# Block-sparse attention with token mix: inner units in pairs with shared keys, edge units of both blocks and four heads, key copies on GpSimd

## The chip, the cores and the metric

The kernel runs on one core of a Trainium2 chip. The metric is the device time of one execution in microseconds (us). Engines are named as in the profile: PE is TensorE, PEld its weight loads, DVE is VectorE, ACT is ScalarE, POOL is GpSimd, SP is the engine that only issues transfers. SBUF is the on-chip memory, PSUM holds the results of PE.

## The reference

Attention over 4 batches, 8 heads, 768 rows in 24 blocks of 32, with a mask by blocks; its result goes through a token mix of dense products.

```python
def _attn_ref(q, k, v, sampled_blocks):          # [4, 8, 768, 64]
    scores = scale * np.matmul(q, k.transpose(0, 1, 3, 2))
    mask = np.abs(blk_i - blk_j) <= 1
    mask = mask | (blk_i == 0) | (blk_j == 0) | (blk_i == 23) | (blk_j == 23)
    for qb in range(24):                         # three sampled blocks for each block of rows
        for kb in sampled_blocks[qb]:
            mask[qb * 32:(qb + 1) * 32, kb * 32:(kb + 1) * 32] = True
    scores = np.where(mask, scores, -1e9)
    attn = np.exp(scores - np.max(scores, axis=-1, keepdims=True))
    attn = attn / (np.sum(attn, axis=-1, keepdims=True) + 1e-09)
    return np.matmul(attn, v)

def _moe_ref(x, w_theta, w_tok_r, w_tok_i, w_ch):   # x: [4, 768, 512]
    theta = x @ w_theta
    yr = np.einsum('ts,bsd->btd', w_tok_r, x * np.cos(theta))
    yi = np.einsum('ts,bsd->btd', w_tok_i, x * np.sin(theta))
    u = x + yr + yi
    return u + np.maximum(u @ w_ch, 0.0)
```

The arrays of the mix arrive as 64-bit words, which the kernel decodes to two float parts each.

## The kernel before

The two batch pairs bp (two batches b each, eight heads as four p and two e) go through attention one after the other. Attention is a list of units. For each bp there are 8 edge units (named w; tiles SW, PW, Tw, XW), whose rows are the first or last block and see all 768 keys, one for each batch, head parity e and edge block z (four heads each); and 22 inner units, one for each other block i. An inner unit covers two batches and eight heads and sees eight key blocks: its own three neighbours, the two edge blocks and three sampled ones.

An inner unit runs through these steps, which the loop over units staggers:

- `gather_k`: copies eight key blocks out of the resident keys kb to the tile kg, scaled by -0.125. ScalarE copies the blocks of the window (L235), VectorE the three sampled ones, at addresses that it reads from a table (L224, L244).
- `scores` (L288): 16 products of 64 rows by 32 columns on PE to S in PSUM, then two reductions to m on VectorE (L291).
- `weights` (L300): four exponentials to P on ScalarE.
- `turn` (L307, L309): eight transpositions to T on PE, and a copy to pT on ScalarE.
- `values` (L318): 32 products of 128 rows by 32 columns to X, 16 with va (the values of the window and of block 0, loaded by SP, L263) and 16 with vb (the sampled values, gathered row by row by an indirect transfer from POOL, L270, and the last block). PE runs each product of full-precision floats as two passes, so the profile counts each twice.
- `finish` (L325 to L328): division by the sum, and a store to xs in DRAM (L341).

Between these, `Decoder` puts one third of a weight piece into each unit: L63 and L80 on ScalarE, L67 to L84 on VectorE. Engines run their instructions in the order written; attention's order is written out by hand in the loop at the end of `attention`. kg has two buffers, vb three, va two, P, pT and X two, T one. `token_mix` begins when attention ends: it reads xs back (xa, xr), and PE bounds it.

Of the kernel before, what the change touches and what calls it, by code (L numbers as in the profile page):

```python
# [12 lines left out]
I32 = mybir.dt.int32  # L13
# [10 lines left out]
VB_BUFS = 3  # L24
Q_AHEAD = 4
# [91 lines left out]
class Tables:  # L117
# [6 lines left out]
    def make(self, nc, cp):  # L124
# [11 lines left out]
        nc.gpsimd.tensor_copy(qi, iota_i)  # L136
        first_i = cp.tile([96, NP], I32, name="first_i")
# [17 lines left out]
        self.rows = rows = cp.tile([96, NP, NB], I32, name="rows")  # L155
# [7 lines left out]
        nc.vector.tensor_scalar(rows, base, ZEROS, None, op0=ALU.add)  # L163


def attention(tc, qT, qE, kT, vr, sampled, xs, ident, pieces, follow):
# [9 lines left out]
    with ExitStack() as ctx, ExitStack() as early:  # L176
# [11 lines left out]
        ps_x = ctx.enter_context(tc.tile_pool(name="ps_x", bufs=2, space=PSUM))  # L188
# [5 lines left out]
        kgs = [gp.tile([P, 8, 8, 32], F32, name=f"kg{x}") for x in range(2)]  # L194
        vas = [cp.tile([P, 1040], F32, name=f"va{x}") for x in range(2)]
# [3 lines left out]
        def load_q(bp, i):  # L199
            if i % 2 == 0:  # L200
                return
            t = qp.tile([P, 2, 2, 4, 32], F32, tag="q", name=f"q{bp}_{i}", bufs=Q_BUFS)
            nc.sync.dma_start(t.rearrange("r u b p f -> r u (b p f)"), qT[bp][:, i - 1 : i + 1, :])
            qbs[bp, i], qbs[bp, i + 1] = t[:, 0], t[:, 1]

        def load_k(bp, b, p0=0, n=4, queue=nc.sync):
            if (b, p0) == (0, 0):
                kbs[bp] = kp.tile([P, 8, NB, 32], F32, tag="kb", name=f"kb{bp}")
            queue.dma_start(kbs[bp][:, 4 * b + p0 : 4 * b + p0 + n], kT[bp, b][:, p0 : p0 + n])

        def load_edges(bp):
            raw = ep.tile([P, 512], F32, tag="qw", name=f"qw{bp}")
            nc.sync.dma_start(raw, qE[bp])
            qes[bp] = raw

        def turn_edges(bp):
            t = ep.tile([P, 2, 2, 4, 32], F32, tag="qe", name=f"qe{bp}")
            nc.vector.tensor_scalar(t.rearrange("r z b p f -> r (z b p f)"), qes[bp], -0.125, None, op0=ALU.mult)
            qes[bp] = t
# [3 lines left out]
        def number_blocks(bp, i):  # L223
            _, numbers[bp, i] = nc.values_load_multi_w_load_instructions(  # L224
                tab.block[0:1, 3 * i : 3 * i + 3], engines=[mybir.EngineType.DVE], min_val=0, max_val=NB - 1,
                skip_runtime_bounds_check_because="Tables clamps the block numbers",
            )

        def gather_k(bp, i):
            kg, kb = kgs[i % 2], kbs[bp]  # L230
            def blocks(b0, n):
                return kb[:, :, b0 : b0 + n, :].rearrange("r g s f -> r s g f")

            def copy(s0, b0, n):
                nc.scalar.activation(kg[:, s0 : s0 + n], blocks(b0, n), AF.Copy, scale=-0.125)  # L235

            if i <= 2:
                copy(3, 0, 1)
                copy(7, NB - 1, 1)
            for b0, n in fresh(i, i <= 2):  # L240
                copy(b0 % 3, b0, n)
            for k, number in enumerate(numbers.pop((bp, i))):
                src = kb[:, :, bass.ds(number, 1), :].rearrange("r g s f -> r s g f")
                nc.vector.tensor_scalar(kg[:, 4 + k : 5 + k], src, -0.125, None, op0=ALU.mult)  # L244
            st[bp, i] = dict(kg=kg)

        def fresh(i, new):

            runs = []
            for blk in range(i - 1 if new else i, i + 2):  # L250
                if runs and blk % 3:
                    runs[-1][1] += 1
                else:
                    runs.append([blk, 1])
            return runs

        def load_window(bp, i):
            va = vas[i % 2]
            if i <= 2:
                nc.sync.dma_start(va[96:128], vr[768 * bp : 768 * bp + 32])  # L260
            for b0, n in fresh(i, i <= 2):
                s0 = 32 * (b0 % 3)
                nc.sync.dma_start(va[s0 : s0 + 32 * n], vr[768 * bp + 32 * b0 : 768 * bp + 32 * (b0 + n)])  # L263
            st[bp, i]["va"] = va

        def gather_v(bp, i):
            vb = vbs[i % VB_BUFS]
            if i <= VB_BUFS:
                nc.sync.dma_start(vb[96:128], vr[768 * bp + 736 : 768 * bp + 768])
            nc.gpsimd.indirect_dma_start(  # L270
                out=vb[0:96],
# [4 lines left out]
            st[bp, i]["vb"] = vb  # L276

        def scores(bp, i):

            s = st[bp, i]  # L280
            q = qbs.pop((bp, i))
            kg = s["kg"]
            sc = ps_s.tile([P, 2, 2, 256], F32, tag="S", name=f"S{bp}_{i}")
            for b in range(2):
                for p in range(4):
                    for e in range(2):
                        rows = slice(64 * e, 64 * e + 64)
                        nc.tensor.matmul(sc[32 * p : 32 * p + 32, e, b, :], q[rows, b, p, :], kg[rows, :, 4 * b + p, :], start=True, stop=True)  # L288
# [13 lines left out]
        def turned(pts, name):  # L302

            n = len(pts)
# [3 lines left out]
            out = wp.tile([P, 8, 128], F32, tag="pT", name=f"pT{name}")  # L308
            nc.scalar.copy(out[:, :n], t[:, :n])  # L309
            return out  # L310

        def turn(bp, i):
            s = st[bp, i]
            s["T"] = turned([s["P"][:, e, b, 128 * c : 128 * c + 128] for c in range(2) for e in range(2) for b in range(2)], f"{bp}_{i}")
# [400 lines left out]
```

## Time and profile before

| | |
|---|---|
| time, median of 3 runs | 638.25 us (636.85 to 638.58) |
| span of the profiled execution | 635.0 us |
| its mean granted clock of PE | 0.964 |
| PE busy over the span | 563.2 us (89%) |
| VectorE | 463.5 us (73%) |
| ScalarE | 361.0 us (57%) |
| GpSimd | 45.6 us (7%) |
| moved by DMA | 96.52 MB, mean 152 GB/s |
| last inner unit's turning copy starts | 286.1 us |

The profile has no time of its own for the execution but its span; the span lies 3.25 us under the median of the runs. A line of groups reads: source line, engine, operation, out<-in, shapes, count, then busy us, mean ns of one, idle us of the engine ahead of it with what ended that. A line in order of time reads: start, us, engine, line, operation, count. Windows are given in us from the start of the span, with busy time and count of each engine, granted clock of PE, share of the 16 DMA engines and GB/s.

### The profile page before, as it was taken

The numbers are of one execution on the slowest core, as the hardware profiler recorded it, in microseconds if no ns is written. First come the engines' busy times: TensorE is split into PE (matmuls) and PEld (weight loads), VectorE is DVE, ScalarE is ACT, GpSimd is POOL, SyncE is SP. The second block draws the span as 40 slices with busy tenths as digits, with TensorE's granted clock in tenths as the row PEclk, the third lists the DMA queues.
The fourth block names the chain that finished last, engine by engine and source line by source line (L and its number), as shares of the span: only waits on it lengthen the run. The fifth ranks groups of instructions, "written<-read, shape, count | busy, mean of one in ns | idle before, by whom it ended". The sixth has DMA issues, their size and how long they took to land.

```text
span 635.0 us, 19148 instructions
## 1 busy us (share of the span) xinstructions
PE 563.2 (89%) x7808; PEld 483.1 (76%) x7808; DVE 463.5 (73%) x1239; ACT 361.0 (57%) x774; POOL 45.6 (7%) x56
## 2 busy tenths in 40 slices
PE   4987778769887768668999999999999999999997
PEld 1555545545455546547999999999999999999997
DVE  1897978875798878758999697575973767746554
ACT  1586768764587767656667564355642465524520
POOL 0101212211002211110000000000000000000000
PEclk9998989988898999887999999999999999999999
DMA  8859979999778997866542224211241211211002
GB/s 287 259 156 246 275 209 259 258 278 345 219 204 244 251 257 226 221 161 170 139 130 73 64 84 143 69 47 50 80 124 59 70 51 42 80 59 61 27 1 99
DMA packets 79959, 96.52 MB, mean 152 GB/s; under 512 B 5312, under 2 KB 64832, under 8 KB 79488
## 3 DMA queue, kind: packets, MB, share of 16 engines
q1 hardware_dynamic: 73088, 72.99, 39.2%
q0 software_dynamic: 4928, 17.57, 10.7%
q10 hardware_dynamic: 1856, 4.74, 2.1%
q8 instruction: 61, 1.00, 0.7%
q14 instruction: 26, 0.21, 0.1%
HBM read 82.70 MB, written 12.58 MB: 150 GB/s over the span
## 4 chain that ended last, share of the span: by engine, by line
PE 66%; DMA 18%; DVE 8%; issue 4%; ACT 2%; SPq 1%; DVEq 1%; ACTq 0%
PE y L555 10%; PE y L556 10%; PE y L557 10%; DMA va<-in_vr_dram 10%; PE X L318 4%; PE S L288 4%; PE T L307 4%; PE h L519 3%; PE h L518 3%; PE o L578 3%; PE h L517 3%; PE o L580 3%; PE o L579 3%; DMA kb<-in_kT_dram 3%; PE SW L357 2%
## 5 line engine op out<-in xcount | busy, mean ns | idle before, releaser
L300 ACT ACTIVATE P<-S,m 128x256 f32<-128x256 f32 x176 | 69.0, 477 | 15.1 <-DVE m L291 14.9
L307 PEld LDWEIGHTS T<-ident,P 128*128 128x128 f32 x352 | 42.1, 150 | 38.2 <-ACT P L300 25.9
L307 PE MATMUL T<-ident,P 128*128 128x128 f32 x352 | 60.5, 304 | 11.2 <-ACT P L300 6.1
L318 PE MATMUL X<-va,pT 128*32 128x65 f32 (+1 forms) x1408 | 50.3, 233 | 21.9 <-DMA va<-in_vr_dram 18.1
L291 DVE TENSOR_REDUCE m<-S 128x2 f32<-128x512 f32 x88 | 56.7, 686 | 16.7 <-PE S L288 9.8
L309 ACT COPY pT<-T 128x1024 f32<-128x1024 f32 x44 | 44.8, 1018 | 41.5 <-PE T L307 41.4
L288 PE MATMUL S<-kg,q 64*32 64x256 f32 x1408 | 55.1, 404 | 10.9 <-issue 10.9
L555 PE MATMUL y<-w_tok_r_hi,zh 128*128 128x384 f32 x192 | 64.6, 336 | 0.0
L556 PE MATMUL y<-w_tok_r_lo,zh 128*128 128x384 f32 x192 | 64.4, 335 | 0.0
L557 PE MATMUL y<-w_tok_r_hi,zl 128*128 128x384 f32 x192 | 64.3, 335 | 0.0
L556 PE MATMUL y<-w_tok_i_lo,zh 128*128 128x384 f32 x192 | 64.2, 334 | 0.0
L555 PE MATMUL y<-w_tok_i_hi,zh 128*128 128x384 f32 x192 | 64.2, 334 | 0.0
L557 PE MATMUL y<-w_tok_i_hi,zl 128*128 128x384 f32 x192 | 62.7, 334 | 0.0
L270 POOL DMA_INDIRECT vb<-in_vr_dram,rows x44 | 44.1, 1002 | 229.3 <-PE X L318 206.0
L318 PEld LDWEIGHTS X<-va,pT 128*32 128x32 f32 (+1 forms) x1408 | 35.6, 116 | 31.8 <-DMA va<-in_vr_dram 17.8
L517 PE MATMUL h<-w_theta_hi,xTh 128*128 128x256 f32 x192 | 55.8, 290 | 1.9 <-ACT xTh L508 1.9
L519 PE MATMUL h<-w_theta_hi,xTl 128*128 128x256 f32 x192 | 55.6, 290 | 0.5 <-DVE xTl L509 0.5
L518 PE MATMUL h<-w_theta_lo,xTh 128*128 128x256 f32 x192 | 55.3, 288 | 0.0
L318 PE MATMUL X<-vb,pT 128*32 128x65 f32 (+1 forms) x1408 | 49.8, 232 | 5.0 <-issue 5.0
L521 ACT ACTIVATE t<-h,up_int 128x256 f32<-128x256 f32 x48 | 22.7, 473 | 42.7 <-PE h L519 42.0
L528 ACT ACTIVATE cs<-rr 128x256 f32<-128x256 f32 x48 | 20.0, 416 | 45.8 <-DVE rr L526 45.8
L578 PE MATMUL o<-uh,w_ch_hi 128*128 128x384 f32 x128 | 42.5, 336 | 0.9 <-DVE of L584 0.9
(125 smaller groups left out, 1337.2 us busy)
## 6 DMA issues: line engine op xcount, KB each, us to landing
xa<-xs SPq DMA_DIRECT2D x192, 64.0 KB
va<-in_vr_dram SPq DMA_DIRECT2D x30, 260.0 KB
xr<-xs SPq DMA_DIRECT2D x24, 256.0 KB
out_dram<-of SPq DMA_DIRECT2D x32, 192.0 KB
q<-in_qT_dram SPq DMA_DIRECT2D x22, 256.0 KB
xs<-xo SPq DMA_DIRECT2D x44, 128.0 KB
vw<-in_vr_dram SPq DMA_DIRECT2D x6, 780.0 KB
raw_tok_r<-in_w_tok_r_dram SPq DMA_DIRECT2D x9, 512.0 KB
```

The lines of the kernel that those rows point to most:

```text
L288: nc.tensor.matmul(sc[32 * p : 32 * p + 32, e, b, :], q[rows, b, p, :], kg[rows, :, 4 * b + p, :], start=True, stop=True)
L291: nc.vector.tensor_reduce(m[:, e], sc[:, e], axis=AX.X, op=ALU.min)
L300: nc.scalar.activation(pt[:, e, b, :], sc[:, e, b, :], AF.Exp, bias=m[:, e, b : b + 1], scale=-1.0)
L307: nc.tensor.transpose(t[:, k, :], pt, ident)
L318: nc.tensor.matmul(x[32 * p : 32 * p + 32, g, :], pt[0:rows, k, 32 * p : 32 * p + 32], v[0:rows, v0 + 65 * p : v0 + 65 * p + 65], start=st ...
L517: nc.tensor.matmul(ps, hi[:, c, :], wh[:, c, :], start=c == 0, stop=False)
L518: nc.tensor.matmul(ps, hi[:, c, :], wl[:, c, :], start=False, stop=False)
L519: nc.tensor.matmul(ps, lo[:, c, :], wh[:, c, :], start=False, stop=c == 3)
L555: nc.tensor.matmul(acc, zh[:, dd], wh[:, j, tt], start=j == 0 and m == 0, stop=False)
L556: nc.tensor.matmul(acc, zh[:, dd], wl[:, j, tt], start=False, stop=False)
L557: nc.tensor.matmul(acc, zl[:, dd], wh[:, j, tt], start=False, stop=j == 5 and m == 1)
L578: nc.tensor.matmul(ps, wh[:, c, :], uh, start=c == 0, stop=False)
```

## The change

Inner units are taken in pairs (i odd, i+1). Four key blocks are shared by the pair: blocks 0, 23, i and i+1. Each unit keeps four of its own: the neighbour that the pair doesn't share and the three sampled ones. kg becomes one tile with two places for shared blocks (used in turn by pairs) and two for own ones (one for each unit of a pair). All key copies go to POOL as plain copies; the scale moves to q (L217, VectorE). The values of a pair are 16 times three products: for each of two units 32 columns with its vb (now 128 gathered rows: sampled blocks and the neighbour), then one product of 64 columns with the shared va. They run once for a pair, in the iteration of the next pair's first unit, and are normalised and stored once for a pair. pT is one tile for both units, without a second buffer; xo has one buffer, vb four; X is two PSUM banks.

An edge unit now has both edge blocks and four heads of one batch: four units for each bp instead of eight. Their scores are products of 64 rows by 64 columns, their values products of 128 rows by 64 columns.

xs is laid out by unit and half of the heads, so that a store writes 2 KB runs; a tile xr is then read by four transfers. Keys are loaded in four parts from SP, for the second batch pair as well. Decoding is spread by weights, two for an edge unit and one for an inner unit.

```diff
+        kg = gp.tile([P, 4, 4, 8, 32], F32, name="kg")
+        pT = gp.tile([P, 2048], F32, name="pT")
...
+        def scale_q(bp, i):
+            if i % 2:
+                t = qbs[bp, i].rearrange("r u b p f -> r (u b p f)")
+                nc.vector.tensor_scalar(t, t, -0.125, None, op0=ALU.mult)
...
         def gather_k(bp, i):
-            kg, kb = kgs[i % 2], kbs[bp]
...
-                nc.scalar.activation(kg[:, s0 : s0 + n], blocks(b0, n), AF.Copy, scale=-0.125)
...
-                nc.vector.tensor_scalar(kg[:, 4 + k : 5 + k], src, -0.125, None, op0=ALU.mult)
+            kb, u, a = kbs[bp], (i - 1) % 2, ((i - 1) // 2) % 2
+            def copy(dst, blocks):
+                nc.gpsimd.tensor_copy(dst, blocks.rearrange("r g s f -> r s g f"))
+
+            if u == 0:
+                if i <= 3:
+                    copy(kg[:, a, 0:2], kb[:, :, 0 : NB : NB - 1, :])
+                copy(kg[:, a, 2:4], kb[:, :, i : i + 2, :])
+            near = i + 1 if u else i - 1
+            copy(kg[:, 2 + u, 3:4], kb[:, :, near : near + 1, :])
+            for k, number in enumerate(numbers.pop((bp, i))):
+                copy(kg[:, 2 + u, k : k + 1], kb[:, :, bass.ds(number, 1), :])
...
+        def load_pair(bp, i):
+            if i % 2 == 0:
+                return
+            va = vas[((i - 1) // 2) % VA_BUFS]
...
+            nc.sync.dma_start(va[64:128], vr[768 * bp + 32 * i : 768 * bp + 32 * (i + 2)])
...
         def gather_v(bp, i):
-                out=vb[0:96],
+                out=vbs[(i - 1) % VB_BUFS],
...
+        def values(bp, i):
+            x = st[bp, i]["X"] = sums_tile(f"{bp}_{i}")
+            va = vas[((i - 1) // 2) % VA_BUFS]
+            order = [(b, e, p) for b in range(2) for e in range(2) for p in range(4)]
+
+            def weigh(b, e, p, c, u0, n, v, start, stop):
+                r0 = 64 * (p % 2) + 32 * u0
+                v0 = 65 * (8 * b + 4 * (p // 2) + 2 * e + p % 2)
+                nc.tensor.matmul(
+                    x[r0 : r0 + 32 * n, b, 2 * (p // 2) + e, :], pT_pair[:, 4 * c + 2 * e + b, p, u0 : u0 + n, :], v[:, v0 : v0 + 65],
+                    start=start, stop=stop,
+                )
+
+            for b, e, p in order:
+                for u in range(2):
+                    weigh(b, e, p, 1, u, 1, vbs[(i - 1 + u) % VB_BUFS], True, False)
+                weigh(b, e, p, 0, 0, 2, va, False, True)
...
+        def values_wide(bp, b, pp, e):
...
+            for c in range(2):
+                for k in range(6):
+                    v0 = 130 * e + 65 * c
+                    nc.tensor.matmul(
+                        x[64 * c : 64 * c + 64, b, 2 * pp + e, :], pT_wide[:, e, k, 64 * c : 64 * c + 64], v[:, k, v0 : v0 + 65],
+                        start=k == 0, stop=k == 5,
+                    )
...
-            nc.sync.dma_start(xr[b, j].rearrange("r i c u -> r i (c u)"), xs[b // 2, b % 2, 4 * j : 4 * j + 4].rearrange("i r c -> r i c"))
+            for p in range(4):
+                src = xs[b // 2, 4 * j : 4 * j + 4, p % 2, :, b % 2, p // 2].rearrange("i q c -> q i c")
+                nc.sync.dma_start(xr[b, j][32 * p : 32 * p + 32].rearrange("r i c u -> r i (c u)"), src)
```

PE, before, around the values of unit 11 of the first batch pair. A row is line, operation, out<-in and the shape of the product's output (rows, which are columns on the array, by 65), xN for N in a row:

```order
L288 MATMUL S_13_1687<-kg_117,q_13_1391 32x256 x16
L307 MATMUL T_12_1707<-ident,P_12_1625 128x128 x8
L318 MATMUL X_11_1727<-va_119,pT_11_1623 32x65 x4
L318 MATMUL X_11_1727<-vb_122,pT_11_1623 32x65 x4
L318 MATMUL X_11_1727<-va_119,pT_11_1623 32x65 x4
```

Now, at the values of the pair 11 and 12 (the three rows of X come 16 times):

```order
L300 MATMUL T_12_1442<-ident,P_12_1378 128x128 x8
L282 MATMUL S_14_1476<-kg,q_13_1128 32x256 x16
L335 MATMUL X_11_1496<-vb_122,pT 32x65
L335 MATMUL X_11_1496<-vb_123,pT 32x65
L335 MATMUL X_11_1496<-va_119,pT 64x65
L335 MATMUL X_11_1496<-vb_122,pT 32x65
```

Groups of four products of one width have become runs of two of 32 and one of 64, and the values stand between the scores and the turning, once for two units.

VectorE, before, from the end of unit 11 to the reduction of unit 14 (ISA rows set an address, TENSOR_LOAD reads block numbers):

```order
L325 TENSOR_SCALAR sm_11_1762<-X_11_1727 128x4
L326 RECIPROCAL sm_11_1762<-sm_11_1762 128x4
L328 TENSOR_TENSOR xo_11_1765<-X_11_1727,sm_11_1762 128x256
L244 ISA
L244 TENSOR_SCALAR kg_117<-kb_131 128x256
L244 ISA
L244 TENSOR_SCALAR kg_117<-kb_131 128x256
L244 ISA
L244 TENSOR_SCALAR kg_117<-kb_131 128x256
L224 TENSOR_LOAD sb_block
L291 TENSOR_REDUCE m_14_1800<-S_14_1783 128x2 x2
```

Now, the same engine at that place:

```order
L217 TENSOR_SCALAR q_15_1293<-q_15_1293 128x512
L285 TENSOR_REDUCE m_14_1493<-S_14_1476 128x2 x2
L75 TENSOR_SCALAR ds_tok_r_1560<-da_tok_r_1420 128x512
L77 SCALAR_TENSOR_TENSOR raw_tok_r_1230<-raw_tok_r_1230,ds_tok_r_1560 128x512
L315 TENSOR_SCALAR sm_11_1563<-X_11_1496 128x8
L316 RECIPROCAL sm_11_1563<-sm_11_1563 128x8
L319 TENSOR_TENSOR xo_11_1566<-X_11_1496,sm_11_1563 128x512
L285 TENSOR_REDUCE m_15_1601<-S_15_1584 128x2 x2
```

The key copies and table reads have left VectorE, a scaling of q has come in ahead of the reduction, and the normalisation stands there once for a pair at twice the width.

POOL, before, in an inner stage has only gathers:

```order
L270 DMA vb_121<-in_vr_dram,rows 96x1040
L270 DMA vb_122<-in_vr_dram,rows 96x1040
L270 DMA vb_120<-in_vr_dram,rows 96x1040
L270 DMA vb_121<-in_vr_dram,rows 96x1040
L270 DMA vb_122<-in_vr_dram,rows 96x1040
```

Now, for the first unit of a pair:

```order
L265 DMA vb_121<-in_vr_dram,rows 128x1040
L243 COPY kg<-kb_128 128x512
L243 COPY kg<-kb_128 128x256
L243 ISA
L243 COPY kg<-kb_128 128x256
L243 ISA
L243 COPY kg<-kb_128 128x256
L243 ISA
L243 COPY kg<-kb_128 128x256
L233 TENSOR_LOAD sb_block
L265 DMA vb_122<-in_vr_dram,rows 128x1040
```

Five copies and a table read have moved in between two gathers, each of which has grown from 96 to 128 rows.

296 lines of the change are left out of this document (157 added, 139 removed).

## The prediction

> **What bounds the kernel now.** I read the span cut at its stages first, because the change touches attention alone.
>
> ```profile
> core 0: us, PE busy (x) PEld busy (x) DVE busy (x) ACT busy (x) POOL busy (x), PEclk, DMA share, GB/s
> 0.00:8.45 8.45, 0.00 (x0) 0.03 (x1) 0.60 (x6) 1.49 (x2) 1.46 (x12) 1.00 0.65 190
> 8.45:43.50 35.05, 33.71 (x576) 17.09 (x576) 25.02 (x64) 19.74 (x31) 2.93 (x3) 1.00 0.80 263
> 43.50:145.60 102.10, 77.57 (x2161) 51.69 (x2153) 81.97 (x218) 73.08 (x149) 19.81 (x19) 0.95 0.91 247
> 145.60:180.70 35.10, 30.65 (x699) 19.22 (x697) 27.42 (x54) 21.55 (x34) 2.74 (x3) 0.90 0.78 261
> 180.70:286.70 106.00, 79.86 (x2208) 55.47 (x2208) 83.06 (x225) 73.84 (x151) 18.62 (x19) 0.91 0.86 227
> 286.70:635.00 348.30, 341.42 (x2181) 339.64 (x2176) 245.46 (x675) 171.27 (x410) 0.00 (x0) 0.99 0.26 78
> ```
>
> The rows are: waiting for keys, edge units of batch pair 0, its 22 inner units, edge units of pair 1, its inner units, token mix. The mix is TensorE at 98%; I leave its 348.3 us alone. In the inner stages (208 us) no engine is above 80%, and the DMA engines are at 86 to 91%. So I read the length of an inner unit from the 22 turning copies of each batch pair, and the chain of waits for what ends last.
>
> ```profile
> L309 ACT COPY pT<-T x22: 1012/1012/1043, 45.5 to 147.6; 128x1024 f32<-128x1024 f32 x22
> L309 ACT COPY pT<-T x22: 1005/1012/1055, 182.6 to 286.1; 128x1024 f32<-128x1024 f32 x22
> ...
> by line: DMA va<-in_vr_dram 24.9%; PE S L288 12.1%; PE X L318 11.9%; PE T L307 8.7%; DMA xs<-xo 8.5%; DMA kb<-in_kT_dram 7.5%; issue 7.5%; DMA raw_tok_r<-in_w_tok_r_dram 5.3%; DVE m L291 3.1%; DVE mw L359 1.5%; PE SW L357 1.3%; PE Tw L307 1
> ```
>
> 102.1 and 103.5 us over 21 steps each: 4.9 us a unit, 9.8 us for two. The chain (52 to 175 us) gives a quarter to the load of the window's values (va). The DMA queues between 90 and 130 us say how full they are:
>
> ```profile
> DMA packets 5068, 9.40 MB, mean 235 GB/s; under 512 B 563, under 2 KB 2778, under 8 KB 5057
> q1 hardware_dynamic: 4161, 6.05, 52.5%
> q0 software_dynamic: 896, 3.20, 31.8%
> ```
>
> These 40 us are 4.1 pairs of units: q1 costs 5.1 us a pair at 288 GB/s, the gather q0 3.1 us at 252 GB/s; 8.2 of 9.8 us. TensorE's part of a unit, once in order of time and once around the changes of product shape:
>
> ```profile
> 95.06 0.30 PE L318 MATMUL X<-va,pT 128*32 128x65 f32 x8
> 95.17 0.30 PE L318 MATMUL X<-vb,pT 128*32 128x65 f32 x8
> 95.40 1.09 PE L288 MATMUL S<-kg,q 64*32 64x256 f32 x32
> ...
> 99.68 1.09 PE L288 MATMUL S<-kg,q 64*32 64x256 f32 x32
> 100.70 1.09 PE L307 MATMUL T<-ident,P 128*128 128x128 f32 x8
> 100.98 0.82 PE L307 MATMUL T<-ident,P 128*128 128x128 f32 x6
> 101.73 0.32 PE L318 MATMUL X<-va,pT 128*32 128x65 f32 x8
> 101.86 0.30 PE L318 MATMUL X<-vb,pT 128*32 128x65 f32 x8
> 101.98 0.30 PE L318 MATMUL X<-va,pT 128*32 128x65 f32 x8
> ...
> L307 PE MATMUL T<-ident,P x176: 272/273/474, 43.5 to 147.1; 128*128 128x128 f32 x176
> L318 PE MATMUL X<-va,pT x88: 217/220/245, 101.7 to 111.9; 128*32 128x65 f32 x88
> ```
>
> Start to start: scores 1.02 us, turning 1.03 us, and the values in groups of four products (two passes each, so x8) every 0.113 us; eight groups and the way back to scores make 1.04. TensorE works 3.1 of 4.9 us. The four products of a group share one 0.113 us because they sit on four different column groups.
>
> **The change, part by part.**
>
> *Values (X), the term that decides.* Before, a pair of units is 16 groups: 2.1 us. Now it is 16 times (two 32-column products, then one 64-column product): 32 steps, and at each the width on the array changes. No row shows 32 beside 64 columns. Bounds:
> - Below: the width costs nothing, and the 64-column product of one head runs beside the 32-column products of the next (other half of the columns): 17 steps of 0.113 = 1.9 us, a gain of 0.2.
> - Above: a change of shape costs what it costs in the rows. T to X (128 to 32 columns, 128 rows both): starts are 0.11 apart within T ((0.82-0.27)/5), the last at 101.53, X starts at 101.73: 0.20, so 0.09 more. X to S (128 to 64 rows): the last pass starts at 95.17+0.30-0.22 = 95.25, S at 95.40: 0.15 where passes follow each other in 0.056; again 0.09 more. And the first group after a change takes 0.13 instead of 0.113. So a step is 0.113 + 0.02 + 0.09 = 0.23 us, with nothing beside it: 32 x 0.23 = 7.4 us, a loss of 5.3.
>
> I take the upper bound: T to X is the nearest row, a change of columns alone, and two kinds of change cost the same 0.09.
>
> The Trainium skill (TensorEngine Tiling (Array Packing), Key Properties) says "Changing tiling mode (not just tile) drains the TensorE", and lists 128x32 and 128x64 as modes of their own; by that rule the upper bound holds. The trace agrees for the two changes above.
>
> *A pair on TensorE*: scores 2 x 1.02, turning 2 x 1.03, values 7.4: 11.5 us, above the old 9.8. The values wait for the second turned copy, and the second turning for the first copy (T and the turned tile have one buffer each); each copy is 1.01 us, with one unit's scores (1.02) beside it, so some 0.2 us shows at each, and I add 0.2 for key copies that come late: **12.1 us**. (12.1-9.8) x 21 pairs = **+48 us**.
>
> *What else an inner pair gains stays hidden under those 12.1 us.* The rows:
>
> ```profile
> L300 ACT ACTIVATE P<-S,m 128x256 f32<-128x256 f32 x87 | 34.2, 477 | 6.9 <-DVE m L291 6.8
> L235 ACT ACTIVATE kg<-kb 128x512 f32<-128x512 f32 x14 | 9.1, 651 | 0.0
> L291 DVE TENSOR_REDUCE m<-S 128x2 f32<-128x512 f32 x42 | 27.0, 686 | 9.9 <-PE S L288 6.8 <-issue 2.0 <-PE T L307 1.1
> L244 DVE TENSOR_SCALAR kg<-kb 128x256 f32 x60 | 13.7, 284 | 0.0
> L328 DVE TENSOR_TENSOR xo<-X,sm 128x256 f32<-128x256 f32 x20 | 8.5, 425 | 0.7
> L68 DVE TENSOR_SCALAR da_tok_r<-da_tok_r 128x512 int32<-128x512 int32 x3 | 1.3, 427 | 0.1
> L69 DVE SCALAR_TENSOR_TENSOR da_tok_r<-raw_tok_r,da_tok_r 128x512 int32<-128x512 int32 x3 | 2.1, 692 | 0.1
> L270 POOL DMA_INDIRECT vb<-in_vr_dram,rows x19 | 19.8, 1042 | 92.0 <-PE X L318 89.8 <-DMA vb<-in_vr_dram,rows 2.2
> L136 POOL CAST qi<-iota_i 128x24 f32<-128x24 int32 x1 | 0.2, 196 | 0.0
> masks.py:197 POOL MEMSET ident<- 128x128 f32 x1 | 0.2, 205 | 0.3 <-POOLq L703 0.3
> ```
>
> - ScalarE loses its key copies (0.65 us a unit). VectorE loses three copies a unit (0.68) and gets one scaling of q a pair (0.43) and one normalisation of twice the width (0.85 for two of 0.42). Decoding goes on at three times 0.43 and four times 0.69 = 4.0 us a piece, 0.79 pieces a pair: 3.2 us. With four reduces (2.7) and the division VectorE has 7.4 us a pair.
> - GpSimd gets nine copies a pair, one of 512 and eight of 256 elements. No row shows one. From the two POOL rows (196 ns at 24 elements, 205 at 128) a lower end is 0.21 each, 1.9 us; from VectorE's copy doubled, 0.57 and 1.14, 5.7 us; I take 0.38 and 0.6, 3.6 us. Each waits for the one before it (0.1), six block numbers are read, and two gathers with 128 rows instead of 96 take 1.04 to 1.39 us: some 8 us a pair, between 5 and 10. Behind these copies stand the gathers, and the scores wait for them; at 12.1 us there is room, at 9 there is little.
> - DMA: gathers 3.1 x 128/96 = 4.1 us; on q1 half of va goes (266 KB at 288 GB/s: -0.9) and a little more weight comes (+0.2): 4.4. Sum 8.5 us, under 12.1. The wait for va goes, since it is loaded two pairs ahead; what is late next is TensorE itself. Stores of attention rows come in runs of 2 KB instead of 512 B; no row prices that, I take nothing.
> - New waits: the scaling of q stands ahead of the reduces on VectorE and waits for a load issued two units before, 9 us at the old pace, more at the new one. The normalised rows have one buffer instead of two, so VectorE waits for the store of the pair before, which has had 12 us. SP issues five transfers a pair where it issued six or seven. These I count at nothing; without their cover (pairs of 9 us beside a full DMA) either could cost some tenths a pair.
>
> *The edge units.* Scores of both heads in one go halve that work (1.4 us per two old units, from the row below); values become 24 serial products, 48 passes of 0.056 = 2.7 us where two old units had 2 x 0.81. Turning stays 2 x 0.81. Sum 5.7 against 6.1 us: I count nothing, bounds -3 and +4 us per stage. The start needs one key piece of 768 KB less: -2 us (0 to -3, at the 190 to 263 GB/s above). Between the batch pairs the chain loses:
>
> ```profile
> 28.78 1.49 PE L357 MATMUL SW<-kb,qe 64*32 64x512 f32 x16
> ...
> 134.78 9.23 DMA kb<-in_kT_dram
> 144.07 10.50 DMA xs<-xo
> 154.67 0.42 DVE xo L328
> ```
>
> Now four smaller key loads stand ahead in one queue with the values loaded before: the 35.1 us become some 29, **-6** (0 to -9). Going over to the mix, each raw tile is four loads instead of one: +1 (0 to +3).
>
> *Sum*: +48 -2 -6 +1 = **+41 us**. The profiled execution spans 635.0 us, 3.25 under the median 638.25 of the runs; I put that on both sides: 638.25 + 41 = **679 us**.
>
> **The rivals.**
> 1. *The change of width costs nothing* (lower bound). Then a pair is bounded by DMA, 8.5 us, or by GpSimd's 8; with the order of waits 9.0. -0.8 x 21 = -17, with the rest -24: **614 us**, faster. For it: DMA wait and key copies, which fill the chain now, do go. Against it: both changes of shape in the trace cost 0.09. It decides below 0.07 us a step beyond the 0.113, or when neighbouring heads overlap.
> 2. *Only one of the two directions costs it*: values 16 x 0.23 + 16 x 0.113 = 5.5 us, pair 10.1; +6 -7: **637 us**, no change.
> 3. *Widths are free, but GpSimd is the bound.* Its copies and VectorE's decode meet: if each of the 3.6 us of VectorE work between SBUF tiles holds GpSimd up, a pair is 8 + 3.6 = 11.6 us: +38 -7: **669 us**; half of it is 9.8 and no change. Against it: the gathers share POOL with the decode now and keep 1.04 us. The Trainium skill (SBUF — State Buffer, Who interferes with whom) states such an exclusive lock between VectorE's two-port modes or two SBUF inputs and GpSimd; no copy on GpSimd is in this trace to show it.
> 4. *All overlaps, and copies are cheap*: VectorE's 7.4 bounds, pair 7.8: **589 us**.
>
> **How the numbers follow.** Forecast 0.62; rivals 0.22, 0.06, 0.05, 0.05. A difference of 0.3% is 1.9 us. Slower: 0.62 + 0.04 + 0.02 = 0.68; faster: 0.22 + 0.05 = 0.27; same 0.05. The forecast's own range is 662 to 696: a pair at 11.5 (no wait shows) to 12.7, edge stages at their bounds. Since rival 1 has over 0.2, the range that holds 8 in 10 goes down to 610: 610 to 696.
>
> **What would show it.** X in the inner stages: starts 0.23 us apart and 7.4 us a pair, TensorE over 90% busy there, copies 6 us apart on average, DMA share falling to 0.7, VectorE waiting for X. If X takes 2 us a pair, the forecast is wrong whatever the end. GpSimd's copies show their price directly; if GpSimd is never idle in the inner stages, rival 3 holds.

## The result, and the profile after

The changed kernel takes 728.41 us (median of 4 runs, 721.82 to 731.15) against 638.29 us: 1.143 times the time before, interval 1.136 to 1.150. It is slower, as forecast, but by 90 us and not by 41, and above the range. The profiled execution spans 728.2 us, 93.2 us more than before. Some executions of a kernel take a few per cent longer at a lower granted clock: the ratios below leave them out and the medians don't, and the profiled executions of fours_one_spread and fours_spread_all were such, so these two have no stage lengths below. The span cut at its stages (columns as in the table of before; start, edge units, inner units, edge units, inner units, mix):

```profile
0.00:7.20 7.20, 1.49 (x8) 0.61 (x12) 0.60 (x6) 1.49 (x2) 1.97 (x16) 1.00 0.61 189
7.20:42.50 35.30, 29.77 (x364) 20.24 (x356) 23.30 (x54) 16.68 (x24) 10.80 (x21) 0.95 0.78 268
42.50:191.00 148.50, 140.81 (x1877) 91.89 (x1875) 90.36 (x154) 65.82 (x126) 58.12 (x109) 0.94 0.61 197
191.00:226.50 35.50, 30.82 (x369) 23.27 (x368) 17.73 (x33) 15.49 (x23) 7.81 (x16) 0.79 0.47 149
226.50:374.00 147.50, 139.69 (x1901) 94.35 (x1898) 92.08 (x167) 70.77 (x140) 54.84 (x102) 0.98 0.52 161
374.00:728.20 354.20, 339.03 (x2088) 335.89 (x2088) 238.11 (x653) 163.57 (x394) 0.00 (x0) 0.99 0.25 75
```

TensorE is now busy 95% of the inner stages and the DMA engines 52 to 61%: the bound has moved from DMA to TensorE, as forecast. For a sum against before, the marks that both kernels share are the 22 turning copies of each batch pair:

```profile
L302 ACT COPY pT<-T x22: 1012/1014/1030, 44.7 to 177.5; 128x1024 f32<-128x1024 f32 x22
L302 ACT COPY pT<-T x22: 991/1014/1029, 228.3 to 364.1; 128x1024 f32<-128x1024 f32 x22
```

| from, to | before | after | difference | forecast |
|---|---|---|---|---|
| start to the first copy | 45.5 | 44.7 | -0.8 | -2 |
| the copies of batch pairs 0 and 1 (inner units) | 102.1 + 103.5 | 132.8 + 135.8 | +63.0 | +48 |
| last copy of pair 0 to first of pair 1 | 35.0 | 50.8 | +15.8 | -6 |
| last copy to the end (hand-over and mix) | 348.9 | 364.1 | +15.2 | +1 |
| sum | 635.0 | 728.2 | +93.2 | +41 |

Two thirds stand in the inner units. One pair of units, in order of time on TensorE:

```profile
71.66 1.09 PE L282 MATMUL S<-kg,q 64*32 64x256 f32 x32
72.69 0.51 PE L335 MATMUL X<-vb,pT 128*32 128x65 f32 x4
...
73.38 0.31 PE L335 MATMUL X<-vb,pT 128*32 128x65 f32 x4
73.62 0.33 PE L335 MATMUL X<-va,pT 128*64 128x65 f32 x2
73.88 0.31 PE L335 MATMUL X<-vb,pT 128*32 128x65 f32 x4
...
80.83 1.09 PE L300 MATMUL T<-ident,P 128*128 128x128 f32 x8
```

Each head starts a 32-column group and then a 64-column one, 0.24 and 0.26 us after the one ahead; 16 heads make 8.15 us, and the pair 12.44 (73.38 here, 85.82 in the next pair). Between the batch pairs and at the hand-over the chain of waits shows what is late (start, length, what):

```profile
160.56 11.77 DMA kb<-in_kT_dram
...
172.46 3.05 PE SW L365 x16
...
182.99 12.34 PE X L335 x96
195.33 1.49 PE Tw L300 x6
```

```profile
374.95 0.23 SPq L348
...
375.22 7.57 DMA xs<-xo
```

The keys of the second batch pair take 11.8 us to land; then the last pair's values take 12.34 us instead of 8.15, since TensorE ran at half clock there (the clock records have one stretch of 30.7 us at 0.5). At the start of the mix the last store of attention rows takes 7.6 us to land, while the DMA engines move little:

```profile
DMA packets 682, 0.53 MB, mean 70 GB/s; under 512 B 65, under 2 KB 553, under 8 KB 681
```

That row is the window 375.2 to 382.8 us. That a store of 256 KB lasts so long while so little else is moved was the clue to the second half of this case.

### The profile page after: what moved, and what is told of

Same layout as the page of the kernel before. It is cut to its first block, busy times and chain, and to the rows that moved or that the text cites. A ratio compares the mean times of both kernels' runs of the same rounds, so it can differ in the third digit from the quotient of the medians.

```text
span 728.2 us, 16678 instructions
## 1 busy us (share of the span) xinstructions
PE 681.6 (94%) x6592; PEld 566.3 (78%) x6592; DVE 462.2 (63%) x1063; ACT 333.8 (46%) x708; POOL 133.5 (18%) x262
## 4 chain that ended last, share of the span: by engine, by line
PE 69%; DMA 12%; DVE 10%; ACT 5%; SPq 2%; issue 2%; DVEq 0%; ACTq 0%
PE X L335 22%; PE y L622 7%; PE y L623 7%; PE y L624 7%; PE T L300 5%; DMA xs<-xo 3%; PE S L282 3%; DMA out_dram<-of 3%; PE SW L365 3%; ACT pT L302 3%; PE h L586 2%; PE h L584 2%; PE h L585 2%; DMA kb<-in_kT_dram 2%; PE o L645 2%; PE o L646 2%
## 5 line engine op out<-in xcount | busy, mean ns | idle before, releaser
L335 PE MATMUL X<-va,pT 128*64 128x65 f32 x704 | 118.4, 251 | 0.0
L335 PE MATMUL X<-vb,pT 128*32 128x65 f32 x1408 | 114.3, 236 | 1.5 <-ACT pT L302 1.1
L243 POOL COPY kg<-kb 128x256 f32 (+2 forms) x202 | 88.2, 477 | 67.8 <-PE S L282 33.8
L335 PEld LDWEIGHTS X<-va,pT 128*64 128x64 f32 x704 | 68.8, 138 | 34.2 <-issue 2.8
L302 ACT COPY pT<-T 128x1024 f32<-128x1024 f32 x44 | 44.6, 1014 | 96.7 <-PE T L300 96.5
L335 PEld LDWEIGHTS X<-vb,pT 128*32 128x32 f32 x1408 | 54.1, 109 | 35.3 <-ACT pT L302 1.3
L584 PE MATMUL h<-w_theta_hi,xTh 128*128 128x256 f32 x192 | 57.2, 298 | 10.5 <-ACT xTh L575 10.5
L300 PE MATMUL T<-ident,P 128*128 128x128 f32 x352 | 49.0, 283 | 4.0 <-ACT pT L302 1.6
L300 PEld LDWEIGHTS T<-ident,P 128*128 128x128 f32 x352 | 38.6, 143 | 15.9 <-ACT pT L302 13.7
L282 PE MATMUL S<-kg,q 64*32 64x256 f32 x1408 | 48.9, 387 | 0.0
L315 DVE TENSOR_SCALAR sm<-X 128x8 f32<-128x8 f32 x22 | 3.6, 165 | 70.1 <-PE X L335 70.1
```

The source lines that it names most:

```text
L243: nc.gpsimd.tensor_copy(dst, blocks.rearrange("r g s f -> r s g f"))
L300: nc.tensor.transpose(t[:, k, :], pt, ident)
L302: nc.scalar.copy(out, t.rearrange("r k (p q) -> r k p q", p=4) if len(out.shape) == 4 else t)
L335: nc.tensor.matmul(x[r0 : r0 + 32 * n, b, 2 * (p // 2) + e, :], pT_pair[:, 4 * c + 2 * e + b, p, u0 : u0 + n, :], v[:, v0 : v0 + 65], star ...
L584: nc.tensor.matmul(ps, hi[:, c, :], wh[:, c, :], start=c == 0, stop=False)
```

## The experiments

Times are medians; a ratio is to the kernel before on the same chip, with its 95% interval. "Inner" is the length from the first to the last turned copy of each batch pair, "end" that from the last copy to the end, both from one profiled execution; X is the length of a pair's values at full clock with no wait inside.

| kernel | time, us | ratio | X | inner | end |
|---|---|---|---|---|---|
| before | 638 | 1 | 2 x 1.04 | 102.1, 103.5 | 348.9 |
| changed | 728.4 | 1.143 (1.136 to 1.150) | 8.15 | 132.8, 135.8 | 364.1 |
| one_width | 692.5 | 1.078 (1.070 to 1.086) | 2.2 | 124.5, 119.3 | 363.8 |
| one_width_fours | 685.0 | 1.068 (1.062 to 1.074) | 2.1 | 123.7, 114.5 | 363.8 |
| two_heads | 688.4 | 1.074 (1.067 to 1.081) | 4.3 | 124.2, 115.6 | 363.6 |
| four_heads | 690.7 | 1.075 (1.068 to 1.082) | 3.1 | 120.3, 119.7 | 366.7 |
| two_buffers | 727.3 | 1.135 (1.122 to 1.148) | 8.15 | 131.6, 134.8 | 368.9 |
| fours_two_buffers | 676.8 | 1.060 (1.052 to 1.067) | 2.1 | 118.1, 109.8 | 363.7 |
| heads_two_buffers | 685.0 | 1.072 (1.064 to 1.080) | 4.3 | 120.4, 114.9 | 365.2 |
| rows_two | 722.0 | 1.133 (1.124 to 1.141) | 8.15 | 132.0, 135.9 | 361.0 |
| fours_q_queue | 680.9 | 1.068 (1.060 to 1.075) | 2.1 | 117.5, 116.8 | 362.1 |
| fours_q_rows | 680.9 | 1.069 (1.062 to 1.077) | 2.1 | 117.7, 111.7 | 364.2 |
| fours_no_gather | 637.4 | 1.003 (0.999 to 1.007) | 2.1 | 94.7, 93.0 | 363.3 |
| fours_four_narrow | 676.4 | 1.061 (1.051 to 1.072) | 2.1 | 117.9, 111.7 | 362.8 |
| fours_spread | 634.6 | 0.988 (0.983 to 0.993) | 2.1 | 102.2, 94.6 | 351.7 |
| heads_spread | 643.8 | 1.006 (1.001 to 1.012) | 4.3 | 97.2, 100.2 | 361.2 |
| after_spread | 711.7 | 1.104 (1.095 to 1.113) | 8.15 | 126.9, 132.3 | 360.8 |
| fours_one_spread | 633.3 | 0.983 (0.969 to 0.998) | | | |
| fours_spread_all | 631.2 | 0.973 (0.962 to 0.984) | | | |

**The widths.** Four kernels differ from the changed one only in the products of `values`. one_width keeps the order of heads and gives each 64-column product as two of 32:

```diff
-                weigh(b, e, p, 0, 0, 2, va, False, True)
+                for u in range(2):
+                    weigh(b, e, p, 0, u, 1, va, False, True)
```

> Each 64-column product of a head becomes two of 32 columns, everything else and the order of heads stay: 64 products a pair instead of 48, and no change of width among them. Theory A (the change of width is the price: the array empties, 0.15 us from the last pass of one width to the first of the other, and the second pass of a product comes 0.08 to 0.11 us late instead of 0.056): the values of a pair fall from 8.15 us to 1.9 to 3.6, the pair from 12.44 to 8.5 to 9.2 where DMA (8) and VectorE (7.6) bound it, the time to 630 to 660 us. Rival B (the price is the order: each head's own products follow one another and wait for the sum in PSUM, whatever the width): values 7 us or more, time 710 to 730. Rival C (GpSimd's copies bound the pair anyway): values 2 to 4, but a pair of 11 us or more, time over 690.

X fell to 2.2 us, so theory A holds for the values and rival B is out: the same order with 16 products more takes a quarter of the time. But the time is 692, neither 630 to 660 nor over 700. These are the numbers of rival C, so something else holds the pair at 11 to 12 us. That it is GpSimd, as rival C said, doesn't fit: in one_width_fours below it is busy for 23.1 of the 40 us from 90 to 130, and fours_spread, further down, has the same copies and is 50 us faster.

one_width_fours takes the same products, two heads at a time (`for b, e, p in order[::2]`: four of vb, then four of va):

> The same products of 32 columns as in one_width, but those of two heads together: four first terms on the four column groups, then four second terms, as before the change. Theory A: values 2.0 us a pair, time 630 to 655 us, within 15 us of one_width. Rival B (order, not width): this one alone is fast, 630 to 655, with one_width 60 us above it.

X 2.1 us, 685.0: within 15 us of one_width, and not under 655 either.

two_heads keeps both widths, with two heads at a time; four_heads takes four (both batches):

```diff
+            for b, e, p in order[::2]:
+                for h in range(2):
+                    for u in range(2):
+                        weigh(b, e, p + h, 1, u, 1, vbs[(i - 1 + u) % VB_BUFS], True, False)
+                for h in range(2):
+                    weigh(b, e, p + h, 0, 0, 2, va, False, True)
```

> Widths stay as changed (32 and 64 columns), but two heads are taken together: four products of 32 columns, then two of 64: 16 changes of width a pair instead of 32. Theory A: values 16 x 0.25 = 4.0 us a pair, TensorE 8.2 of it, pair about 9 us; time 640 to 665. Rival B: the products of one head still follow one another, but two heads side by side: about the same 4 us, so this run tells A from B only by its passes (0.15 us at each change of width). Rival C: pair over 11, time over 690.

> As two_heads with four heads together (two batches): eight products of 32 columns, then four of 64: 8 changes of width a pair, and as many products as in two_heads. Theory A: 8 changes fewer at 0.10 us each take 0.8 us off the values: about 3.0 us a pair; the pair, if bounded by DMA and VectorE, hardly moves: time 0 to 15 us below two_heads. Rival B: the number of changes does not matter, values as in two_heads.

X is 4.3 us with 16 changes of width a pair and 3.1 with 8: with the same 48 products, 8 changes fewer save 1.2 us, 0.15 each (0.10 was expected). Halving or removing X leaves the time at 685 to 691 all the same. In one_width_fours the waits between 205 and 300 us (engine and line, what it waited for: total, times, longest) show the new place:

```profile
DVE xo L319 <- DMA xs<-xo: 23.6, 7, 4.6
```

VectorE waited for the store of the pair before: the single row buffer, a wait that the prediction had counted at nothing.

**The single buffer.** Three kernels get two buffers (`bufs=1` to `bufs=2` for xo; to make room the scratch of the block tables lies in the second window tile): the changed one, one_width_fours and two_heads.

> The changed kernel with two buffers for the normalised rows (xo) instead of one, and nothing else but where the block tables' scratch lies (in the second window tile, to make room). Theory A (a pair is bound by TensorE, 12.44 us with 8.15 of values; the wait for the store of the pair before shows only where the pace is broken, 5.8 us in all): pair stays 12.4, time 715 to 728. Rival D (the store wait sets the pace here as well): pair falls below 11.5, time under 705.

> one_width_fours (products of 32 columns alone, four side by side: values 2 us a pair) with two buffers for the normalised rows. There VectorE waited 11.8 us in 40 for the store of the pair before, and the pair took 11.1 us instead of 9. Theory A' (two prices, one hidden behind the other: the widths, and behind them the single buffer whose store takes 8 to 10 us): pair 8.5 to 9.5, time 632 to 655. Rival C (GpSimd's copies, locked out by VectorE, or DMA bound the pair): pair 10.5 or more, time over 670.

> two_heads (32 and 64 columns, two heads at a time, 16 changes of width a pair) with two buffers for the normalised rows. Theory A': values 4 us, TensorE 8.2 us a pair plus its waits for the copies: pair 9 to 10, time 640 to 668, some 5 to 20 us above fours_two_buffers. Rival C: as fours_two_buffers and over 670.

Theory A held for the changed kernel (727.3, no gain to speak of), but theory A' failed: 676.8 and 685.0, with pairs of 10.5 to 11.5 us (a stage is 10.5 pairs). The wait for the store is gone and others stand in its place. In fours_two_buffers the chain of waits has the values at 2.1 us, so X is not what is long, and between 44 and 150 us the waits have

```profile
48.09 2.11 PE X L336 x128
```

```profile
DVE q L218 <- DMA q<-in_qT_dram: 25.1, 6, 10.2
```

and the window as a whole:

```profile
core 0: us, PE busy (x) PEld busy (x) DVE busy (x) ACT busy (x) POOL busy (x), PEclk, DMA share, GB/s
44.00:150.00 106.00, 75.40 (x2080) 55.11 (x2066) 72.97 (x135) 58.39 (x116) 58.91 (x100) 0.87 0.73 226
```

**One queue, or all engines?** fours_q_queue sends the loads of q from ScalarE's queue (`nc.sync.dma_start` to `nc.scalar.dma_start` in `load_q`); fours_no_gather skips the gathers after the first four of a batch pair.

> fours_two_buffers (no change of width, two buffers for the rows) takes 675 to 677 us and 10.5 us a pair; VectorE waits 38 us there to scale q, for loads that take up to 11.8 us to land behind 1.3 MB of other loads in SP's one queue. Here the loads of q alone go from ScalarE's queue. Theory Q (the order of one queue sets the pace): the waits for q go, pair 9.5 to 9.8, time 655 to 665. Rival R (the DMA engines' throughput sets it, 2.25 MB a pair): another load is late instead, pair 10.2 or more, time 670 to 680.

> fours_two_buffers without the gathers of sampled values after the first four of each batch pair (the products use old rows): 1.06 of 2.25 MB a pair less, on GpSimd's own queue; SP's queue stays as it is. Theory R (throughput of the DMA engines): pair under 9, time 630 to 650. Theory Q (order and waits in SP's queue): its loads still stand behind one another but pass faster when nothing shares the engines; pair 9.5 to 10.2, time 655 to 668. Neither (waits among the engines, half-speed TensorE): 670 to 677.

With q on its own queue its waits go, and TensorE waits for va instead, 24.0 us between 44 and 150 us where it was 14.6; no gain (680.9). In fours_q_queue the waits of that window have the first of these lines. The chain of waits has the others: SP issues the two transfers of a store (L352), and the load of va right behind them takes 16.3 us to land:

```profile
PE X L336 <- DMA va<-in_vr_dram: 24.0, 5, 7.8
```

```profile
96.56 0.51 SPq L352
...
97.12 0.48 SPq L352
...
97.70 16.28 DMA va<-in_vr_dram
```

Without the gathers the inner stages fall to 94.7 and 93.0 us. Theory R (throughput) fits both, except for one number: the engines were busy 0.73 in the mean, where before they stood at 0.91, and at about that share a load of 260 KB took 16.3 us. The records of single packets say more. In fours_q_queue the 128 packets of a pair's store (2 KB each, the only ones of that size in SP's queue there) come at 1 to 26 a microsecond, 208 of them from 95 to 113 us, while up to 72 gather packets a microsecond go by. With nothing beside it, in the changed kernel at 377 to 382 us, the order is plain: two chains, in each of which a packet starts 0.080 us after the one ahead; 64 x 0.080 = 5.1 us. The store of the kernel before, with nothing beside it at 297.4 us, started some 90 packets of 512 B in 0.16 us. The records don't name the engine of a packet, but two such chains are what a store on two of the 16 engines would give.

The code has the 2: the store's outermost dimension is the two blocks of a pair (`u q b p f -> u q (b p f)`), where before it was 128 rows (`b r c -> r b c`). The Trainium skill (DMA: Bandwidth & Descriptors, "Why a DMA increments its semaphore by 16 and not by 1", on how many engines) states this: the slowest dimension that isn't 1 decides, and a transfer uses the largest number of engines up to 16 that divides it on both sides; for transfers of this kind always the lowest-numbered ones. The two chains agree with the first part; which engines they are, no run here shows.

**The store, spread.** fours_spread stores the same bytes in four transfers of 32 rows:

```diff
-                nc.sync.dma_start(xs[bp, i : i + 2, c].rearrange("u q b p f -> u q (b p f)"), xo[64 * c : 64 * c + 64])
+                for u in range(2):
+                    r0 = 64 * c + 32 * u
+                    nc.sync.dma_start(xs[bp, i + u, c].rearrange("q b p f -> q (b p f)"), xo[r0 : r0 + 32])
```

> fours_two_buffers, where the rows of a pair are stored in four transfers whose outermost dimension is 32 rows, instead of two whose outermost dimension is 2 (the blocks of the pair), the same bytes in the same runs of 2 KB. Theory E (a store with an outermost dimension of 2 runs on two DMA engines, 64 packets of 0.080 us each = 5.1 us a pair on those two, above the 6.8 us that every engine has of the other transfers: 11.9 us, which is what bounds a pair; all loads behind it wait for these two): pair 8.5 to 9.3, time 640 to 655. Rival R (throughput of all engines): no change, 670 to 678.

> heads_two_buffers (products of 32 and 64 columns, 16 changes of width a pair; 685 us) with the same four stores. Theory E: pair 9 to 9.6, where TensorE's 8.2 and the waits for the two copies bound it; time 648 to 662, 5 to 15 us above fours_spread. Rival R: 680 to 687.

> The changed kernel with the four stores and nothing else. The pair stays 12.4 us, since TensorE bounds it (values 8.15). Theory E: the last store, which takes 7.6 us to land at the opening of the mix, lands in about 2.5, and the loads behind it are no longer held: stage from the last turned copy to the end 364 to about 359, between the batch pairs 1 to 5 us less; time 712 to 723. Rival R: 722 to 731.

All three came out as theory E said and not as rival R, with times just below its ranges (634.6 for 640 to 655, 643.8 for 648 to 662, 711.7 for 712 to 723). fours_spread takes 634.6 us, 42 less than fours_two_buffers and 1.2% less than the kernel before. Between 44 and 140 us its engines, and its waits for va and q, are:

```profile
44.00:140.00 96.00, 73.60 (x1971) 51.90 (x1974) 69.08 (x130) 56.04 (x111) 54.45 (x98) 0.86 0.84 251
```

```profile
PE X L336 <- DMA va<-in_vr_dram: 1.2, 1, 1.2
...
DVE q L218 <- DMA q<-in_qT_dram: 6.2, 1, 6.2
```

0.84 busy and 251 GB/s where 0.73 and 226 stood, and the waits for va and q are down to 1.2 and 6.2 us: the loads no longer stand behind a store that takes long. TensorE's granted clock is the same in both windows, 0.87 and 0.86, so it isn't what made the difference. The sum of theory E is not exact, though: 11.9 us is more than the 10.5 to 11.2 us a pair that fours_two_buffers takes, so how full the two engines were is not shown. heads_spread, with 16 changes of width, is at 643.8, 9 us above. In the changed kernel, where TensorE bounds the pair, the store costs 17 us (728.4 to 711.7, on two chips). The two profiles differ by 13.6 us: 9 of them stand at the ends of the inner stages, 3 at the hand-over.

Two things had changed in fours_spread, and the buffer was still open. fours_four_narrow also has four transfers, but split by batch, so that each keeps its outermost 2; fours_one_spread has the spread store with one buffer.

> As fours_spread four transfers a pair, but split by batch, so that each keeps the outermost dimension of 2 blocks (64 rows in runs of 1 KB). Theory E (two DMA engines carry such a store, whatever the number of transfers): as slow as fours_two_buffers, pair 10 us or more, time 665 to 690. Rival F (the number or size of the transfers made the difference): as fours_spread, 630 to 640.

> fours_spread with one buffer for the normalised rows, as in the change. Theory E (the buffer is harmless once a store is spread over all engines and lands in 3 to 4 us, well before the next pair's rows): 630 to 642, within 1% of fours_spread. Rival G (the single buffer is a cost of its own): 645 to 665.

676.4 and 633.3: the number of transfers does nothing, the outermost dimension all; and the single buffer costs nothing once a store is quick. In fours_four_narrow the window of 44 to 140 us has the clock of fours_spread, but the DMA share and rate of fours_two_buffers:

```profile
44.00:140.00 96.00, 66.09 (x1868) 48.71 (x1866) 64.75 (x119) 51.94 (x103) 56.77 (x93) 0.86 0.70 225
```

Against the changed kernel, the widths alone give 43 us (one_width_fours), the store alone 17, both 95 (fours_one_spread); by the ratios, each of which has its own chip's kernel before, it is 48, 25 and 102. Either way both give more than the sum of the two: each hid part of the other.

**The hand-over.** rows_two is the changed kernel and loads each raw tile of the mix in two transfers instead of four; fours_q_rows is fours_q_queue and does so from GpSimd's queue; fours_spread_all is fours_spread with edge rows in transfers of 32 rows and the loads of rows_two.

```diff
-            for p in range(4):
-                src = xs[b // 2, 4 * j : 4 * j + 4, p % 2, :, b % 2, p // 2].rearrange("i q c -> q i c")
+            for g in range(2):
+                src = xs[b // 2, 4 * j : 4 * j + 4, :, :, b % 2, g].rearrange("i c q f -> (c q) i f")
```

> The changed kernel, where the mix loads each of its raw row tiles in two transfers of 64 partitions instead of four of 32: 48 loads instead of 96. From the last turned copy to the end the changed kernel takes 364 us where it took 349. Theory M (what is lost there is the queue: four loads at 0.43 to 0.5 us each to issue stand ahead of one another and of the gathers of the rotated tiles): 4 to 10 us less, time 715 to 726. Rival N (the rows are late because the last pair's values take 8 us and its store is last, whatever the number of loads): no change, 722 to 731.

> fours_q_queue, and the mix's raw row tiles come in two transfers each from GpSimd's queue, which is idle in the mix, instead of four each from SP's. All kernels with the change take 361 to 367 us from the last turned copy to the end, before 349. Theory M (SP's queue of row loads makes the opening of the mix late): that stage falls by 8 to 12 us, to 352 to 356, time 8 to 12 below fours_q_queue. Rival N (the opening is late by the order in which the engines' work stands, rows or no): the stage stays over 360.

> fours_spread, with the edge rows stored in transfers of 32 rows as well and the mix's raw tiles loaded in two transfers instead of four. Theory E: between the batch pairs and in the opening of the mix 2 to 8 us less together, time 632 to 650. Rival: within 3 us of fours_spread.

By its time rows_two would fit theory M (722.0, though its interval overlaps that of the changed kernel). But its end is 361.0 against 364.1, 3 us less where M said 4 to 10, and two_buffers, whose mix is that of the changed kernel, has 368.9, so 3 us are within what single executions differ by. In the profiles 6 us of its gain stand ahead of the loads, between the batch pairs (44.6 where the changed kernel has 50.8). With the loads on an idle queue the end is 364.2, against 362.1 in fours_q_queue, and the time is the same: nothing speaks for theory M.

The end is shortest with the spread store: 351.7 in fours_spread, 12 less than in fours_two_buffers with all else equal. Only half of that is waiting saved: from the last copy on, TensorE is idle for 11.2 us instead of 17.4. Its busy time falls as well, from 346.3 to 340.5 us for the same products, with a granted clock of 0.99 instead of 0.97 over that stage. Where the clock stays (0.98 from heads_two_buffers to heads_spread, 0.99 from the changed kernel to after_spread), the same edit takes 3 to 4 us off the end (361.2, 360.8). Why the clock was better in that execution is not settled. fours_spread_all has the lowest time, 0.973 of the time before (0.962 to 0.984); its gain over fours_spread is not clear of the spread of either.

## Why the prediction was wrong

*The deciding term was right in kind and near in size.* The values take 8.15 us a pair where 7.4 was forecast: a step is 0.25 us on average, not 0.23, because at full clock the last pass is 0.15 us ahead of the next width, and a product's second pass comes 0.08 (32 columns) or 0.11 us (64) after its first, instead of 0.056. The pair is 12.44 (forecast 12.1), TensorE 95% busy, DMA at 0.6. The ten pairs between the first and the last copies make (12.44 - 9.72) x 10 = 27 us a stage, 54 in both; the forecast had 48. The other 9 of the 63 stand at the ends of the stages, and with the store spread they are gone: in after_spread the inner stages are 9.4 us shorter together, and the last copy of batch pair 0 comes 2.5 us after the one ahead, where in the changed kernel it comes 8.1 us after it, behind edge scores that wait for their keys. The rule of the Trainium skill on changes of tiling mode (TensorEngine Tiling (Array Packing), Key Properties), weighed there, agrees with these rows: 0.15 us at a change where passes of one width follow in 0.056, and 8 changes fewer saved 1.2 us.

*Two steps failed. By size the first is the pair of terms for the ends of the stages, -6 and +1: they came out at +15.8 and +15.2, which is 36 of the 52 us that the sum of +41 lacks to +93.2.* The two paragraphs on these stages, below, say what stood there.

*The second is one sentence: "Stores of attention rows come in runs of 2 KB instead of 512 B; no row prices that, I take nothing."* The diff shows a store whose outermost dimension went from 128 to 2, and the prediction weighed the length of the runs alone. It cost 17 us in the changed kernel. It is also why rival 1 was mispriced: without any cost of the widths the time is not 614 but 685 (one_width_fours), and with the store spread too, 634.6. The DMA term "sum 8.5 us, under 12.1" added up bytes over 16 engines; by the two chains of packets, the store alone took 5.1 us a pair on two of them.

*The new waits, counted at nothing, were the places where it showed.* The row buffer and the scaling of q did wait, for 24 and 25 us in windows of 95 and 106 us, once X was short: 2 to 3 us a pair, where the text said some tenths. Neither was a cost of its own: with the store spread, one buffer does no harm (fours_one_spread) and the wait for q is 6.2 us. In the changed kernel X covered them, as the text had said for the pace of 12 us.

*Between the batch pairs -6 was forecast and +15.8 came.* The eleventh pair's values fall into this stage, which the text left out: 8.15 us where a single unit's 1.04 stood, 7 us. With X short, in one_width and one_width_fours, the stage is 38.1 and 38.8 us. Some 6 us more belong to this execution: TensorE ran at half clock for 30.7 us, which made the values 12.34 us and the scores and the turning beside them slow too. In rows_two, whose attention is the same, the values take 8.1 us there and the stage 44.6, with a granted clock of 0.89 instead of 0.72. And the keys in four loads took 11.8 us to land where the chain of before had 9.2; TensorE waited 3.1 us for them, and not at all in after_spread.

*The hand-over: +1 was forecast for four loads instead of one; +15.2 came.* From the last copy on, TensorE is busy for 347.0 us where it was 342.0: here too the last pair's values, 8.0 us, stand where a unit's stood. And it is idle for 17.1 us where it was 6.9, above all for rows that come late; the first line is from before, the second from now:

```profile
PE h L517 <- ACT xTh L508: 1.9, 1, 1.9
```

```profile
PE h L584 <- ACT xTh L575: 10.5, 5, 2.5
```

The last store lands late (7.6 us), but with the store spread the end is only 3 us shorter, as it is with half as many loads. Most of this idle time stays open.

*GpSimd's copies were priced somewhat low.* 0.38 and 0.6 us were taken, 3.6 us a pair; between 60 and 150 us the changed kernel shows some 0.42 and 0.81 us, 4.1 a pair:

```profile
L243 POOL COPY kg<-kb 128x256 f32 x45 | 18.9, 454 | 0.0
L243 POOL COPY kg<-kb 128x256 f32<-128x256 f32 x15 | 6.0, 399 | 0.0
L243 POOL COPY kg<-kb 128x512 f32<-128x512 f32 x8 | 6.5, 810 | 0.0
```

GpSimd was idle half of the time, so rival 3 did not happen as stated. Its mechanism is there on the other side: some of VectorE's operations on two SBUF inputs, 0.69 us in the kernel before, are stretched:

```profile
L84 DVE TENSOR_TENSOR w_theta_lo<-da_theta,raw_theta 128x512 fp32r<-128x512 f32 x2 | 4.0, 2010 | 0.1
L77 DVE SCALAR_TENSOR_TENSOR raw_tok_r<-raw_tok_r,ds_tok_r 128x512 f32<-128x512 uint32 x3 | 3.4, 1132 | 0.1
```

Of these five operations the three that begin during one of GpSimd's copies take 2.0 us each, and the two that meet none 0.69. The lock that the Trainium skill states (SBUF — State Buffer, Who interferes with whom) agrees with these rows; VectorE had the room.

## What to carry to other kernels

When a diff changes the layout of a transfer, read its outermost dimension on both sides before its bytes and runs: it decided here how fast the transfer ran (634.6 us with 32 rows outermost, 676.8 with 2), and a mean DMA share of 0.73 hid that the loads waited behind it. The ends of a stage need a sum of their own: what is done once for a pair stands there alone, without the next pair's work beside it. A cost that is found and removed shows what stood behind it, so a rival that says "this term costs nothing" needs its own bound worked out term by term, and a term without a row is not zero. On TensorE it paid to collect products by tile width: four heads together kept the wide products at 3.1 us where head by head took 8.15.

## What the runs showed of the hardware that was not expected

- A store whose outermost dimension is 2 ran as two chains of packets of 2 KB, one every 0.080 us in each: 5.1 us for 64 packets, and 7.6 us to land with little else under way. Loads behind it in the same queue took up to 16.3 us to land, and moving the loads of q to another queue did not help.
- A change between products of 32 and 64 columns takes 0.15 us from the last pass to the first of the new width, in both directions, and 8 of them fewer a pair saved 0.15 us each.
- Products of 32 columns of neighbouring heads overlap even when each head's four stand in a row (one_width, 2.2 us for 64 products).
